# Gated mix of sliding attention and a GEGLU block: two staging tiles moved from ring s to rings s and c

## The chip, the cores and the metric

The kernel runs on one core of a Trainium2 chip. The metric is the device time of one execution in microseconds, as the median of several runs; one more execution is taken by the hardware profiler. Five engines work side by side and meet at semaphores: TensorE (PE), VectorE (DVE), ScalarE (ACT), GpSimd (POOL) and SyncE (SP), the last of which here only issues DMAs.

## The reference

The inputs are x (2048 tokens of 512 channels), weights for attention and for a gated feed-forward block (FFN), and a gate vector:

```python
def _A_ref(x, wqkv, wo):          # 32 heads of 16, 8 keys per token, every second token back
    qkv = ...(x @ wqkv)
    idx = pos[:, None] - (jnp.arange(8) * 2)[None, :]
    logits = jnp.einsum("bhsd,bhswd->bhsw", q, k[..., idx, :]) * scale   # masked where idx < 0
    attn = softmax(logits)
    return (einsum("bhsw,bhswd->bhsd", attn, v[..., idx, :])) @ wo
def _B_ref(x, w_gate, w_up, w_down):   # 512 -> 1792 -> 512
    return (_gelu(x @ w_gate) * (x @ w_up)) @ w_down
g = _sigmoid((x * gate_w).sum(-1, keepdims=True))
return g * a + (1 - g) * b
```

## The kernel before

Tokens are split by parity (`par` 0 and 1), since the attention looks back by even steps only: two problems of 1024 tokens. Every matrix product is made in full precision from three products of high and low parts, and with a two-by-two block scheme that saves multiplications at the price of sums between the blocks (the names `a11`, `b21`, `t3`, `s4` and so on are blocks and sums of blocks).

For each parity the program first makes keys and queries, then runs `ffn(par)`: fourteen blocks `f` of 128 hidden channels. `gate_up` makes the gate and the up product of a block (L558 on PE), `hidden` multiplies them and splits the product into the high part `hh` and the low part `hl` (L572, L574, L575), and `down` (L601) multiplies those with the down weights `d`. The operands `g0` and `g1` of a block are split into high and low parts by ACT (L515, L520) with a subtraction by a POOL DMA (L516); `d` by L544, L545 and L547, for the first two blocks by `down_split` (L117 and DVE).

The product with the value weights, `values(par)`, has no stage of its own: its steps are cut into the first two FFN blocks, in the order that the table `PLAN` gives. It works by token tiles `t` of 0 to 3. Each makes two sets of 128 rows of values (`jj = t` and `jj = BT + t`), 512 channels wide, in two halves of 256. ACT (L224) and DVE (L232) gather each set in one tile of 512 columns in SBUF, and two DMAs write it to memory, its first half by L228 (on ACT's queue for par 0, on SP's for par 1) and its second half by L233 (on SP's queue). The table `STAGES` says from which ring each of these tiles is taken: `STAGES[t][0]` for the first set, `STAGES[t][1]` for the second.

A ring is a small set of equal buffers under one name, handed out in turn: a new tile waits until every reader of the tile that had its buffer is done, DMAs included. The rings `s` and `c` have four buffers each. `c` tiles are 544 columns wide, `s` tiles 512. Each FFN block takes two tiles of `s`, the copies of `p5` and `u2` out of PSUM (`copy`, L563), and four of `c`: the gelu of the first half (`c11`, L656), the sums `c12` and `c22` (`add`, L568), and the gelu of the second half (`ge`, L675).

The attention runs on DVE beside all of this (scores L324 and L327, softmax L344 to L368, mix L386 to L401), fed in between the FFN steps by `pull`. Its results go through memory and come back by L806, are split by L87 and L88, and are multiplied with the output weights (L828) at the end. The end of the program is a run of L828 matmuls.

The order of the instructions on each engine is not the order of the text: a scheduler takes the whole program, estimates when each instruction could run, and writes out the order of each engine; it hands out the ring buffers as it goes. A ring that is changed can move instructions on all engines.

Of the kernel before, what the change touches and what calls it, by code (L numbers as in the profile page):

```python
# [48 lines left out]
def tile_gated_mix(ctx: ExitStack, tc: tile.TileContext, xt, wqkv, wff, wo, out):  # L49
# [11 lines left out]
    def tl(tag, dt=F32):  # L61
        return pool.tile([P, COLS.get(tag, 512)], dt, name=tag, bufs=BUFS[tag])
# [14 lines left out]
    for i in range(WARM):  # L77
        c = i // 4 % 2 * QW
# [115 lines left out]
            VR["t4"] = VR["b21"]  # L194
            sub(VR["t4"], VR["b21"], VR["t2"])

    STAGES = (("r", "r"), ("hh", "hl"), ("s", "s"), ("s", "s"))

    def value_steps(par, t):

# [14 lines left out]
        def staged(i):  # L215
            if ("s", i) not in T:
                T["s", i] = tl(STAGES[t][i])[:, :512]
            return T["s", i]
# [1188 lines left out]
```

## Time and profile before

| what | value |
|---|---|
| median of 3 runs | 606.85 us (605.4 to 607.78) |
| the profiled execution | 601.95 us |
| its span | 600.2 us |
| PE busy | 587.3 us (98%), 2730 matmuls |
| DVE busy | 540.0 us (90%) |
| ACT busy | 391.2 us (65%) |
| POOL busy | 89.2 us (15%) |

A profile line of the timeline reads: start in us, duration, engine, line of the program, operation, output<-input, shapes, count, and in brackets the time that the engine was idle before it and what ended that. In a list of waits the columns are the total, the number of times and the longest. Several consecutive instructions of one kind are one line. The duration given for PE is from the start of the first to the modelled end of the last; matmuls overlap, so that the start of the next line is the better mark.

### The profile page before, as it was taken

The page shows a single profiled execution, that of the slowest core. Times are in us where ns is not written, and L with a number is a line of the kernel's source. Part 1 is how long each engine was busy: PE and PEld are TensorE (multiplying, and loading weights), DVE is VectorE, ACT ScalarE, POOL GpSimd, SP SyncE. Part 2 cuts the span into 40 slices and gives each one's busy share as a digit, 9 for nine tenths or more (in the row PEclk, how much of TensorE's full clock was granted, in tenths as well). Part 3 has the DMA queues.
Part 4 walks back from the last instruction along what each step waited for, and adds up shares of the span by engine and source line. Part 5 has one row for each costly group of instructions (what it writes and reads, how often), then busy time and mean ns, then how long its engine had stood idle before and what let it go on. Part 6 is the DMA issues. An engine that isn't in the chain of part 4 may idle for free.

```text
span 600.2 us, 8102 instructions
## 1 busy us (share of the span) xinstructions
PE 587.3 (98%) x2730; PEld 488.1 (81%) x2730; DVE 540.0 (90%) x644; ACT 391.2 (65%) x678; POOL 89.2 (15%) x121
## 2 busy tenths in 40 slices
PE   8999999999999999999899999999999999999997
PEld 6888978878887888877788888788888888888886
DVE  5998989879999899989989999899999899799972
ACT  5857646787776967785874346768666766785532
POOL 0501002111211111201117000111111111101200
PEclk9999999999999999999999999999999999999999
DMA  8778969898999799896779886877798587737824
GB/s 315 245 233 235 297 195 254 226 287 225 258 254 283 199 274 239 225 331 243 229 220 274 241 211 183 225 210 181 192 236 261 146 219 219 225 95 203 128 66 158
DMA packets 79810, 134.18 MB, mean 224 GB/s; under 512 B 7964, under 2 KB 45210, under 8 KB 79512
## 3 DMA queue, kind: packets, MB, share of 16 engines
q1 hardware_dynamic: 64426, 98.72, 50.0%
q0 software_dynamic: 12576, 32.97, 28.2%
q10 hardware_dynamic: 2766, 1.96, 1.0%
q8 instruction: 21, 0.34, 0.2%
q14 instruction: 21, 0.17, 0.1%
HBM read 68.30 MB, written 38.86 MB: 179 GB/s over the span
## 4 chain that ended last, share of the span: by engine, by line
PE 86%; DMA 5%; issue 4%; ACT 2%; DVE 2%; POOL 0%; SPq 0%; DVEq 0%; POOLq 0%; ACTq 0%
PE p L558 40%; PE p L601 11%; PE acc L601 10%; PE acc L895 7%; PE p L895 5%; PE p L828 5%; PE acc L210 5%; PE acc L828 2%; DMA g<-raw 2%; DMA vs<-s 1%; DMA d<-r 1%; DMA raw<-xt 1%; ACT L675 0%; ACT L344 0%; DVE prod L386 0%
## 5 line engine op out<-in xcount | busy, mean ns | idle before, releaser
L558 PE MATMUL p<-S,g 128*128 128x512 f32 x672 | 168.9, 390 | 3.7 <-ACT s L563 2.7
L558 PEld LDWEIGHTS p<-S,g 128*128 128x128 f32 x672 | 125.0, 188 | 30.3 <-ACT s L563 3.4
L558 PE MATMUL p<-A,g 128*128 128x512 f32 x504 | 128.9, 390 | 1.1 <-DMA g<-raw 0.5
L558 PEld LDWEIGHTS p<-A,g 128*128 128x128 f32 x504 | 93.6, 188 | 21.3 <-DVE c L568 1.2
L327 DVE TENSOR_REDUCE lg<-prod 128x128 f32<-128x2048 f32 x32 | 73.0, 2281 | 0.1
L516 POOL DMA_DIRECT2D g<-raw x40 | 34.5, 862 | 227.7 <-ACT g L515 134.0
L601 PE MATMUL p<-d,hh 128*128 128x512 f32 x224 | 67.4, 389 | 0.0
L601 PE MATMUL acc<-d,hh 128*128 128x512 f32 x224 | 62.1, 390 | 0.7 <-DMA d<-r 0.7
L386 DVE TENSOR_TENSOR prod<-kq,lg 128x2048 f32<-128x2048 f32 x24 | 54.7, 2277 | 0.2
L601 PEld LDWEIGHTS acc<-d,hh 128*128 128x128 f32 x224 | 41.8, 188 | 9.7 <-DMA d<-r 1.1
L601 PEld LDWEIGHTS p<-d,hh 128*128 128x128 f32 x224 | 42.1, 188 | 8.8
L563 ACT ACTIVATE s<-p 128x512 f32<-128x512 f32 x56 | 32.9, 597 | 22.9 <-PE p L558 18.8
L520 ACT ACTIVATE g<-raw 128x1024 fp32r<-128x1024 f32 (+1 forms) x40 | 39.5, 987 | 12.1 <-PE p L558 9.4
L515 ACT ACTIVATE g<-raw 128x1024 fp32r<-128x1024 f32 (+1 forms) x40 | 39.3, 986 | 10.3 <-PE p L895 6.3
L545 POOL DMA_DIRECT2D d<-r x24 | 20.5, 855 | 147.0 <-ACT d L544 120.1
L601 PE MATMUL p<-d,hl 128*128 128x512 f32 x112 | 41.8, 389 | 0.0
L574 ACT ACTIVATE hh<-c 128x512 fp32r<-128x512 f32 x56 | 35.1, 628 | 9.9 <-DVE c L572 9.9
L575 DVE TENSOR_TENSOR hl<-c,hh 128x512 fp32r<-128x512 f32 x56 | 38.3, 683 | 3.7 <-ACT hh L574 3.6
L568 DVE TENSOR_TENSOR c<-p,s 128x512 f32<-128x512 f32 x56 | 38.1, 683 | 3.8 <-PE p L558 2.8
L572 DVE TENSOR_TENSOR c<-c 128x512 f32<-128x512 f32 x56 | 38.2, 682 | 2.2 <-ACT c L675 2.1
L617 ACT ACTIVATE rt<-p 128x512 f32<-128x512 f32 x48 | 27.7, 595 | 18.6 <-PE p L601 18.0
L390 DVE TENSOR_TENSOR prod<-prod 128x1024 f32<-128x1024 f32 x32 | 38.9, 1216 | 0.1
(203 smaller groups left out, 1016.0 us busy)
## 6 DMA issues: line engine op xcount, KB each, us to landing
g<-raw POOLq DMA_DIRECT2D x27, 512.0 KB, 6.1
raw<-wff SPq DMA_DIRECT2D x42, 256.0 KB, 4.0
ws<-g SPq DMA_DIRECT2D x14, 768.0 KB, 5.7
g<-ws SPq DMA_DIRECT2D x14, 768.0 KB, 5.3
r<-wff SPq DMA_DIRECT2D x28, 256.0 KB, 4.2
d<-r POOLq DMA_DIRECT2D x24, 256.0 KB, 6.2
g<-raw POOLq DMA_DIRECT2D x13, 384.0 KB, 6.3
os<-tb SPq DMA_DIRECT2D x64, 64.0 KB, 4.3
```

The lines of the kernel that those rows point to most:

```text
L327: nc.vector.tensor_reduce(two_of(lg, jj), prod.rearrange("p j w (h d) -> p (j w) h d", d=DH), axis=AX.X, op=OP.add)
L386: paced(nc.vector.tensor_tensor(prod.rearrange("p j w (h d) -> p (j w) h d", d=DH), spans(v, jj).rearrange("p j w (h d) -> p j w h d", d=D ...
L390: nc.vector.tensor_tensor(prod[:, :, :4], prod[:, :, :4], prod[:, :, 4:], op=OP.add)
L515: nc.scalar.activation(lo, raw, AF.Copy, scale=-1.0)
L520: ins = nc.scalar.activation(hi, raw, AF.Copy)
L558: LAST[:] = [nc.tensor.matmul(ps, w_, a_, start=(start and kc == 0 and n == 0), stop=(kc == 1 and n == 2), skip_group_check=True)]
L568: nc.vector.tensor_tensor(c, ps, s, op=OP.add)
L572: nc.vector.tensor_tensor(ge, ge, up, op=OP.mult)
L575: nc.vector.tensor_tensor(hl_, ge, hh_.bitcast(F32), op=OP.subtract)
L601: ins = nc.tensor.matmul(pp, a[:, ts], w, start=(i == 0 and n == 0 and gr == 0), stop=(i == 1 and n == 2), skip_group_check=True)
L828: ins = nc.tensor.matmul(pa, a, b, start=(first and n == 0), stop=(last and n == 2), skip_group_check=True)
L895: return lambda *args, **kw: self.add(getattr(self.eng, name)(*args, **kw))
```

## The change

Token tile 2 takes its first tile from `s` and its second from `c`; token tile 3 its first from `c` and its second from `s`. Both took both from `s`.

```diff
-    STAGES = (("r", "r"), ("hh", "hl"), ("s", "s"), ("s", "s"))
+    STAGES = (("r", "r"), ("hh", "hl"), ("s", "c"), ("c", "s"))
```

The instructions are the same in kind and number. Their order differs on every engine from 74 us on. Three places follow; numbers behind a name tell the tiles of one name apart, `[waits ...]` names the engines or DMA queues on which an instruction waits.

The first place is in par 0, between blocks 1 and 2. On PE, `p_847` and `p_888` belong to block 1, `p_1035` to block 2, `acc0` to `acc3` to the values or to `down`; the names behind `<-` are the operands. Before, block 1's matmuls from `S_247` stood behind the first of block 2, from `g0_842`:

```order
L558 MATMUL p_1035<-A_118,g0_842 128x512 [waits Activation_49]
L558 MATMUL p_1035<-A_118,g0_842 128x512
L558 MATMUL p_1035<-A_118,g0_842 128x512 [waits DMASW2_49]
L558 MATMUL p_1035<-A_119,g0_842 128x512 x3
L558 MATMUL p_847<-S_247,g1_708 128x512 [waits Activation_49]
L558 MATMUL p_847<-S_247,g1_708 128x512 x2
L558 MATMUL p_847<-S_248,g1_708 128x512 x3
L601 MATMUL acc0_1050<-d_952,hh_798 128x512 [waits PE_49,Activation_49]
L601 MATMUL acc0_1050<-d_952,hh_798 128x512
```

Now they stand 30 rows earlier, straight behind those from `S_245`:

```order
L558 MATMUL p_888<-S_245,g1_708 128x512 [waits Activation_49]
L558 MATMUL p_888<-S_245,g1_708 128x512 x2
L558 MATMUL p_888<-S_246,g1_708 128x512 x3
L558 MATMUL p_847<-S_247,g1_708 128x512 [waits Activation_49]
L558 MATMUL p_847<-S_247,g1_708 128x512 x2
L558 MATMUL p_847<-S_248,g1_708 128x512 x3
L210 MATMUL acc0_775<-hh_468,S_247 128x256 [waits Activation_49]
L210 MATMUL acc0_775<-hh_468,S_247 128x256
```

On ACT at the same place, `s_895` and `s_939` are the copies `p5` and `u2` of block 1, `s_808`, `s_929`, `s_836` and `s_948` stage tiles. Before, `g0_842` (the high part of block 2's operand) stood ahead of `s_939`, and `s_939` and the first eviction into `s_948` waited for DMAs:

```order
L224 ACTIVATE s_929<-acc3_876 128x256 [waits PE_49]
L117 ACTIVATE d_952<-r_785 128x512 [waits PE_49]
L117 ACTIVATE d_955<-r_838 128x512 [waits DMAHW6_49]
L520 ACTIVATE g0_842<-raw_632 128x768
L563 ACTIVATE s_939<-p_847 128x512 [waits DMAHW6_49,DMAHW3_49,DVE_49]
L224 ACTIVATE s_836<-acc0_775 128x256 [waits DVE_49,PE_49]
L224 ACTIVATE z_113<-acc0_775 128x1
L228 DMA vs00_86<-s_836 128x2x128 [waits DMAHW2_49,Activation_49]
L638 ACTIVATE p_1042<-p_1035 128x512 [waits PE_49]
L224 ACTIVATE s_948<-acc2_941 128x256 [waits DMAHW7_49,DMAHW2_49]
```

Now the stage tiles are `s_808`, `c_836`, `c_929` and `s_948`; the gelu `c_907` is the `ge` of block 0, `c_965` the `c11` of block 1. In two pieces, a little apart:

```order
L675 ACTIVATE c_907<-p_594 128x512
L515 ACTIVATE g1_897<-raw_632 128x1024 [waits DVE_49]
L228 DMA vs00_86<-hl_729 128x2x128 [waits DMAHW1_49,Activation_49]
L224 ACTIVATE s_808<-acc1_782 128x256 [waits PE_49]
L224 ACTIVATE z_113<-acc1_782 128x1
L563 ACTIVATE s_895<-p_888 128x512
L563 ACTIVATE s_939<-p_847 128x512
```

```order
L574 ACTIVATE hh_910<-c_907 128x512 [waits DVE_49]
L224 ACTIVATE acc1_883<-acc3_876 128x258 [waits PE_49,Activation_49]
L224 ACTIVATE c_929<-acc1_883 128x256 [waits PE_49]
L224 ACTIVATE z_113<-acc1_883 128x1
L656 ACTIVATE c_965<-p_854 128x512
L228 DMA vs00_86<-c_929 128x2x128 [waits DMAHW7_49,Activation_49]
L224 ACTIVATE s_948<-acc2_941 128x256 [waits PE_49]
L117 ACTIVATE d_952<-r_785 128x512 [waits DMAHW3_49]
L117 ACTIVATE d_955<-r_838 128x512
L520 ACTIVATE g0_842<-raw_632 128x768
```

The two L563 copies stand one behind the other and wait for no DMA; ahead of the L520 copy of `g0_842` stand `s_939` and `s_948`. Further on come `c_1076`, the `ge` of block 1, and `c_1111`, the `c11` of block 2, both with waits for DMAs that read the stage tiles whose buffers they take:

```order
L675 ACTIVATE c_1076<-p_847 128x512 [waits DMAHW1_49,DMAHW0_49,PE_49]
L515 ACTIVATE g1_1091<-raw_885 128x1024 [waits DMAHW4_49,DMASW1_49,DVE_49]
L656 ACTIVATE c_1111<-p_1042 128x512 [waits DMAHW7_49,DMAHW6_49]
L520 ACTIVATE g1_1091<-raw_885 128x1024
L228 DMA vs00_86<-s_948 128x2x128 [waits Activation_49]
```

The second place is on ACT towards the end of par 0, at 254 us of the profile before: an exp of the attention (L344) with its table load, a gelu (L675) with another, and the L638 copy of `p_2530`, for which PE waits there. Before:

```order
L895 ACTIVATE A_2550<-raw_2384 128x512 [waits DMAHW6_49,PE_49]
L544 ACTIVATE d_2532<-r_2382 128x512 [waits PE_49]
L895 ACTIVATE A_2552<-raw_2384 128x512
L344 ACT_TABLE_LOAD
L344 ACTIVATE lg_2204<-lg_2204 128x512 [waits DVE_49]
L675 ACT_TABLE_LOAD
L675 ACTIVATE c_2565<-p_2389 128x512 [waits PE_49]
L638 ACTIVATE p_2530<-p_2523 128x512 [waits Activation_49]
L617 ACTIVATE rt_1133<-p_2473 128x512 [waits PE_49]
L617 ACTIVATE rt_1157<-p_2502 128x512 [waits PE_49]
```

Now:

```order
L547 ACTIVATE d_2532<-r_2382 128x512 [waits DMAHW4_49,DMASW1_49,PE_49]
L344 ACT_TABLE_LOAD
L344 ACTIVATE lg_2204<-lg_2204 128x512 [waits DVE_49]
L617 ACTIVATE rt_1133<-p_2473 128x512 [waits PE_49]
L617 ACTIVATE rt_1157<-p_2502 128x512 [waits PE_49,Activation_49]
L895 ACTIVATE A_2550<-raw_2384 128x512 [waits DMAHW6_49,PE_49]
L638 ACTIVATE p_2530<-p_2523 128x512 [waits PE_49,Activation_49]
L544 ACTIVATE d_2532<-r_2382 128x512
L895 ACTIVATE A_2552<-raw_2384 128x512
L675 ACT_TABLE_LOAD
L675 ACTIVATE c_2565<-p_2389 128x512 [waits PE_49]
```

The exp stands ahead of the copies into `A`, and the gelu with its table load behind the L638 copy.

The third place is on PE at the change of parity, at 282 us of the profile before. `p<-d` are the last matmuls of `down`, whose results ACT evicts by L612; `acc<-g_2556` and `p<-g_2593` are the first products of keys and queries of par 1 (L895). Before:

```order
L601 MATMUL p<-d,hh 128x512 x2
L601 MATMUL p<-d,hl 128x512
L895 MATMUL acc_2796<-g_2556,A 128x512 x6
L895 MATMUL acc_2797<-g_2556,A 128x512 x6
L895 MATMUL acc_2798<-g_2556,A 128x512 x6
L601 MATMUL p<-d,hh 128x512 x8
L895 MATMUL acc_2799<-g_2556,A 128x512 x6
L601 MATMUL p<-d,hl 128x512 x4
L895 MATMUL p<-g_2593,A 128x512 x5
L895 MATMUL p<-c,A 128x512
```

Now:

```order
L601 MATMUL p<-d,hh 128x512 x8
L601 MATMUL p<-d,hl 128x512 x4
L895 MATMUL acc_2796<-g_2556,A 128x512 x6
L895 MATMUL acc_2797<-g_2556,A 128x512 x6
L895 MATMUL acc_2798<-g_2556,A 128x512 x6
L895 MATMUL acc_2799<-g_2556,A 128x512 x6
L895 MATMUL p<-g_2593,A 128x512 x5
L895 MATMUL p<-c,A 128x512
```

The twelve `p<-d` matmuls stand ahead of the 24 of `acc<-g_2556`, and no longer between them and `p<-g_2593`.

In par 1 the first place is repeated with SP in place of ACT as the queue of the L228 DMAs. There the L568 sums `c_3605` and `c_3711` on DVE carry waits for DMAs that read stage tiles, and the L563 copies beside the stages carry none.

## Prediction

> **What bounds the kernel now.** I read the busy times first, then what TensorE (PE) waited for, then the timeline around each of those waits, and last the final microseconds. From the page, PE's waits (total, times, longest), one stretch of the stages table, and the chain's last pieces:
>
> ```profile
> PE 587.3 (98%) x2730; PEld 488.1 (81%) x2730; DVE 540.0 (90%) x644; ACT 391.2 (65%) x678; POOL 89.2 (15%) x121
> ...
> PE p L558 <- ACT s L563: 2.7, 2, 1.5
> PE p L895 <- ACT p L895: 2.3, 1, 2.3
> ...
> PE p L558 <- ACT p L638: 0.9, 1, 0.9
> PE acc L601 <- DMA d<-r: 0.7, 1, 0.7
> PE p L558 <- DMA g<-raw: 0.5, 1, 0.5
> PE p L558 <- DVE c L568: 0.5, 1, 0.5
> ...
> 60.00:110.00 50.00, 48.53 (x267) 41.86 (x266) 46.38 (x51) 30.07 (x58) 6.80 (x8) 1.00 0.89 248
> ...
> 585.71 5.44 PE acc L828 x24
> 591.14 5.45 PE p L828 x24
> ```
>
> PE is the bound: 24 matmuls of 512 columns take 5.44 us in the last row but one, 0.2267 each, and the granted clock is 1.00 even in the stretch with the longest ring wait. So PE's sum of matmuls is fixed, and the change can act only on the few gaps between them. It adds and removes no instruction. The first wait in the list, 2.7 us in two places, is the one that ring s causes: an L563 copy into s that waits for a stage's DMA.
>
> I size each gap by starts: start of a group plus its matmuls at 0.2267 (0.12 for 256 columns, 356.13 to 356.85 below) is when PE would be free; the next start less that is what was lost. The first half of the sequence (par 0), with ACT beside it:
>
> ```profile
> 80.50 1.61 PE L558 MATMUL p<-A,g 128*128 128x512 f32 x6
> 83.58 1.65 PE L558 MATMUL p<-S,g 128*128 128x512 f32 x6 [1.47 <-ACT s L563]
> ...
> 79.57 0.83 ACT L520 ACTIVATE g<-raw 128x768 fp32r<-128x768 f32 x1
> 82.92 0.60 ACT L563 ACTIVATE s<-p 128x512 f32<-128x512 f32 x1 [2.53 <-DMA vs<-s]
> 83.42 0.38 ACT L224 ACTIVATE s<-acc 128x256 f32<-128x256 f32 x1
> 83.83 0.37 ACTq L228 DMA_DIRECT2D vs<-s  x1
> ...
> 76.39 6.43 DMA vs<-s
> ```
>
> Free at 80.50 + 6 x 0.2267 = 81.86, started at 83.58: 1.72 lost. The copy sat 2.53 us until a stage DMA of 6.43 us had left the buffer. The other gaps that the new order touches:
>
> ```profile
> 132.79 0.84 PE L558 MATMUL p<-A,g 128*128 128x512 f32 x3
> 134.16 1.19 PE L558 MATMUL p<-A,g 128*128 128x512 f32 x4 [0.53 <-DVE c L568]
> ...
> 192.32 0.61 PE L558 MATMUL p<-A,g 128*128 128x512 f32 x2
> 193.47 0.73 PE L558 MATMUL p<-A,g 128*128 128x512 f32 x2 [0.54 <-DMA g<-raw]
> ...
> 257.54 0.84 PE L601 MATMUL acc<-d,hl 128*128 128x512 f32 x3
> 259.33 1.66 PE L558 MATMUL p<-S,g 128*128 128x512 f32 x6 [0.95 <-ACT p L638]
> ...
> 283.88 1.07 PE L601 MATMUL p<-d,hl 128*128 128x512 f32 x4
> 287.26 0.96 PE L895 MATMUL p<-g,A 128*128 128x512 f32 x3 [2.32 <-ACT p L895]
> ...
> 356.13 0.89 PE L210 MATMUL acc<-d,S 128*128 128x258 f32 x6
> 356.85 0.87 PE L210 MATMUL acc<-rt,S 128*128 128x256 f32 x6
> 358.99 1.65 PE L558 MATMUL p<-S,g 128*128 128x512 f32 x6 [1.27 <-ACT s L563]
> ...
> 380.36 1.07 PE L601 MATMUL acc<-d,hh 128*128 128x512 f32 x4
> 382.12 1.21 PE L601 MATMUL acc<-d,hh 128*128 128x512 f32 x4 [0.70 <-DMA d<-r]
> ```
>
> By the same arithmetic they lost 0.69 (at 133), 0.70 (192), 1.11 (258), 2.47 (284), 1.42 (357, the second ring-s wait, par 1) and 0.85 (381). With the 1.72 that is 8.96 us, the most that this change could ever take away.
>
> **The change part by part.** All terms are against the profiled execution: 601.95 us, 0.8% below the median of 606.85, so the sum is scaled by 606.85 / 601.95 at the end.
>
> *Ring s, par 0.* Four stage tiles took all four s buffers; now two do. The two L563 copies of block 1, s_895 and s_939, carry no DMA wait any more and stand side by side on ACT, and the six matmuls p_847<-S_247 have moved 30 rows forward on PE. The 1.72 goes. What is late next is the hi copy of g0_842 (L520), which the matmuls p_1035 wait for. It ended at 79.57 + 0.83 = 80.40, just ahead of PE's 80.50, so it has no cover. In the new row one L563 copy (0.60) and one L224 eviction (0.38) stand ahead of it that did not, and another L224 eviction (0.38) has gone behind. Bounds of the new gap: 0 if ACT's idle time there takes them up, 1.7 if it costs what the old wait did. I take 1.0, near 0.60 + 0.38, since the eviction ahead waits on PE itself. Net -0.72.
>
> *Ring c, par 0.* Stage tiles c_836 and c_929 now hold the buffers that the gelu outputs c_1076 (L675, block 1) and c_1111 (L656, block 2) take next, and these two wait for the stages' DMAs. The spread of such transfers (issue to landing: min, median, max, first of L233 and then of L228), and when the two gelus ran before:
>
> ```profile
> DMA to landing us min/median/max: 1.8/4.8/9.5
> ...
> DMA to landing us min/median/max: 2.0/4.1/8.9
> ...
> 91.73 0.60 ACT L675 ACTIVATE c<-p 128x512 f32<-128x512 f32 x1 [0.38 <-PE p L558]
> ```
>
> The last DMA from that tile went out at 83.83; a median landing frees the buffer at 87.9, the longest at 92.7, 1.0 us after the gelu wants it; an operand copy like that of 79.57, but wider, stands ahead of the DMA now, about one more. Cost taken 0, because the median still leaves nearly 3 us; bounds 0 and 2.0.
>
> *Par 1.* The 1.42 goes in the same way. There the stages' second-half DMAs are all on SP, in a new order, and the L568 sums c_3605 and c_3711 on DVE wait for them; behind those on DVE stand hidden products for PE. Bounds 0 (median landing) and 1.7 (what the old wait cost in par 0). I take a third of the wait that is replaced, 0.5, since these DMAs queue behind loads on SP. Net -0.92.
>
> *The rows in between.* The scheduler hands out the changed rings and gives PE, ACT and DVE another order from 74 us to the end of par 0 and again in par 1. At 284 the twelve matmuls into p from d have moved ahead of the 24 of acc<-g_2556. PE waited for ACT there:
>
> ```profile
> 284.30 2.42 ACT L612 ACTIVATE rt<-p,gc 128x512 f32<-128x512 f32 x4 [3.82 <-PE p L601]
> 286.60 1.09 ACT L895 ACTIVATE p<-acc 128x512 f32<-128x512 f32 x2
> ...
> 254.83 1.28 ACT L344 ACT_TABLE_LOAD   x1
> ...
> 256.78 1.28 ACT L675 ACT_TABLE_LOAD   x1
> 258.70 0.58 ACT L638 ACTIVATE p<-p 128x512 f32<-128x512 f32 x1
> ```
>
> Four evictions (2.42) and half of 1.09 make 2.96, now under 24 x 0.2267 = 5.44 of matmuls: the 2.47 goes, -2.47. Bounds 0 and -2.47. At 258 the exp and its table load stand earlier, and the second load (1.28) and its gelu come after the L638 copy on which PE waited: -1.11, bounds 0 and -1.11. At 381 the L544 copy that starts the late DMA stands earlier on ACT: -0.85, bounds 0 and -0.85. The gaps at 133 and 192 I could not place in the new order: 0, bounds 0 and -1.39. Against this, a new order makes gaps of its own. The old one had two of about 0.7 in this stretch that no ring explains (133, 192), so I charge two more at 0.75: +1.5, bounds 0 and +3.0.
>
> *The end.* PE's last 24 matmuls, at 591.14, need the last attention tile:
>
> ```profile
> 588.42 0.69 DVE L88 TENSOR_TENSOR hl<-raw,hh 128x512 fp32r<-128x512 f32 x1 [6.50 <-ACT hh L87]
> ...
> 345.00:583.00 238.00, 236.04 (x1076) 196.22 (x1075) 221.82 (x240) 153.65 (x254) 28.32 (x34) 1.00 0.72 188
> ```
>
> It is ready at 589.11, 2.0 us early. So of the terms so far (-0.72 - 0.92 - 2.47 - 1.11 - 0.85 + 1.5 = -4.57) only 2.0 is free; the other 2.6 must be made good by DVE, which is idle 238.00 - 221.82 = 16.2 us from 345 on, in part behind PE. I take two thirds made good: +0.9 lost, bounds 0 and 2.6.
>
> Sum: -4.57 + 0.9 = -3.67, 598.28 us, and scaled to the median 603.1.
>
> [...]
>
> **The rivals.** (1) No difference: the attention chain on DVE does not come earlier, so the last tile is ready at 589.11 as before and the end gains only 2.0: 599.95, scaled 604.8. For it speaks DVE's 90%; against it, that DVE also waits on PE. The change not doing what it says, the ring wait merely moved, ends here as well: 284 and 258 alone are 3.58, less 1.5 of new gaps, 604.8 again.
> (2) Slower: ring c. It carries four tiles per FFN block where s carries two, and its gelus stand in ACT's row with the operand copies behind them. With a landing of 9.5 for 6.43, a wait like the old one costs PE 1.72 + 3.07 = 4.8. Two of the four new waits at that size make +9.6 on -4.17: 607.4, scaled 612.3. It decides from about 7.2 us of such waits (4.17 and the 3.0 that can be told), one and a half of them. Against it stand the medians above.
> [...]
>
> **How the numbers follow.** Forecast 0.52, rival 1 0.31, rival 2 0.17. A measurement of this kernel can tell about 0.5%, 3.0 us, from no change, and the three cases are the three outcomes: faster 0.52, same 0.31, slower 0.17. The time is the forecast's 603.1. The low end, 599.0, is the forecast without charge for new gaps, par-1 waits and the end (-6.57, scaled 600.2) and most of 133 and 192 besides; the high end, 609.0, takes in rival 1 and the milder half of rival 2.
>
> **What would show it.** Right: PE's waits name no L563 with a stage DMA behind it; no gap of 2.3 at the L895 copies near 284; L520 of g0_842 starts after PE has come to p_1035. Wrong: L675, L656 or L568 into c waiting on vs<-c; the last tile's hl with PE idle before the final 24 matmuls; several new gaps over 1 us between 85 and 400.

## The result

The changed kernel takes 599.97 us (median of 4 runs, 597.96 to 601.31) against 606.42 (605.40 to 607.78): ratio 0.9889, 95% interval 0.9854 to 0.9924. In a second comparison it was 599.40 against 604.10: 0.9943, 0.9920 to 0.9966. So it is faster, by 4.7 to 6.5 us as the medians have it and by 3.4 to 6.7 us as the ratios have it; 603.1 was forecast, a ratio of 0.9938 to the 606.85 it started from. Spreads, medians and mean clocks below are over all runs, while the ratios leave out those more than 1.5% above the fastest of their kernel. A ratio is not the quotient of two medians of the table: for tile 2 only, where they differ most, that quotient is 0.9925.

The profiled executions differ far less, 599.73 against 601.95. The page of after, and all that PE waited for:

```profile
PE 587.9 (98%) x2730; PEld 489.8 (82%) x2730; DVE 538.9 (90%) x644; ACT 392.0 (66%) x678; POOL 89.4 (15%) x121
...
PE acc L601 <- DMA d<-r: 1.9, 1, 1.9
PE acc L210 <- ACT acc L224: 1.1, 1, 1.1
PE p L79 <- DVE zero L73: 1.1, 1, 1.1
PE p L558 <- ACT p L638: 0.9, 1, 0.9
PE p L558 <- DVE c L568: 0.9, 2, 0.5
PE acc L895 <- DVE A L895: 0.4, 1, 0.4
PE p L558 <- ACT g L520: 0.2, 1, 0.2
```

No L563 and no L895 copy is left in the list; every wait but the two of the start is in a new place. Their places in the timeline of after, three rows of ACT at 381 us, and the waits of an L563 copy in ring s on ACT and of a sum in ring c on DVE:

```profile
82.59 0.39 PE L601 MATMUL acc<-d,hh 128*128 128x512 f32 x1
83.22 0.96 PE L558 MATMUL p<-A,g 128*128 128x512 f32 x3 [0.24 <-ACT g L520]
...
105.23 0.61 PE L601 MATMUL p<-d,hl 128*128 128x512 f32 x2
107.75 0.97 PE L601 MATMUL acc<-d,hh 128*128 128x512 f32 x3 [1.91 <-DMA d<-r]
...
268.87 0.39 PE L601 MATMUL p<-d,hl 128*128 128x512 f32 x1
269.80 1.43 PE L558 MATMUL p<-A,g 128*128 128x512 f32 x5 [0.54 <-DVE c L568]
...
319.28 0.64 PE L210 MATMUL acc<-d,A 128*128 128x258 f32 x4
320.99 0.99 PE L210 MATMUL acc<-d,S 128*128 128x258 f32 x6 [1.08 <-ACT acc L224]
...
379.30 1.07 PE L601 MATMUL acc<-d,hl 128*128 128x512 f32 x4
381.27 0.98 PE L558 MATMUL p<-S,g 128*128 128x512 f32 x3 [0.90 <-ACT p L638]
...
378.80 1.28 ACT L344 ACT_TABLE_LOAD   x1
380.10 0.63 ACT L344 ACTIVATE lg<-lg 128x512 f32<-128x512 f32 x1
380.64 0.58 ACT L638 ACTIVATE p<-p 128x512 f32<-128x512 f32 x1
...
525.83 1.29 PE L558 MATMUL p<-A,g 128*128 128x512 f32 x5
527.45 0.73 PE L558 MATMUL p<-A,g 128*128 128x512 f32 x2 [0.32 <-DVE c L568]
...
360.01 1.09 ACT L563 ACTIVATE s<-p 128x512 f32<-128x512 f32 x2 [0.69 <-DMA vs<-s]
360.42 0.69 DVE L568 TENSOR_TENSOR c<-p,s 128x512 f32<-128x512 f32 x1 [1.30 <-DMA vs<-c]
```

By starts, as in the prediction, these gaps are 0.40 (at 83), 2.07 (105), 0.70 (269), 1.23 (320), 1.06 (381) and 0.49 (527): 5.95 us in place of 8.96, or 3.0 less. The profiled executions differ by 2.2, since after's first 60 matmuls, which the change leaves alone, took 1.5 us longer this time: eight of them stood 0.43 us apart from 6.7 us on, behind a gap of only 0.5 us, though the granted clock reads 1.00 there. Why was not tried. The second profile of after, 598.91 us, lies 3.0 below the first of before.

So the traces leave 1.7 to 3.5 us of the medians unexplained. Two things were open: why before's runs lie so far above its profile, and whether the gain belongs to the rings or to the order.

### The profile page after: what moved, and what is told of

Same layout as the page of the kernel before. It is cut to its first block, busy times and chain, and to the rows that moved or that the text cites. A ratio compares the mean times of both kernels' runs of the same rounds, so it can differ in the third digit from the quotient of the medians.

```text
span 597.9 us, 8098 instructions
## 1 busy us (share of the span) xinstructions
PE 587.9 (98%) x2730; PEld 489.8 (82%) x2730; DVE 538.9 (90%) x644; ACT 392.0 (66%) x678; POOL 89.4 (15%) x121
## 4 chain that ended last, share of the span: by engine, by line
PE 90%; DVE 3%; DMA 2%; ACT 2%; issue 2%; POOL 0%; SPq 0%; POOLq 0%; ACTq 0%; DVEq 0%
PE p L558 41%; PE p L601 11%; PE acc L601 11%; PE acc L895 8%; PE acc L210 6%; PE p L895 5%; PE p L828 5%; PE acc L828 2%; DMA d<-r 1%; DMA raw<-xt 1%; DVE prod L386 1%; DVE prod L390 1%; DVE A L895 0%; DVE c L568 0%; DVE c L572 0%
## 5 line engine op out<-in xcount | busy, mean ns | idle before, releaser
L520 ACT ACTIVATE g<-raw 128x1024 fp32r<-128x1024 f32 (+1 forms) x40 | 39.6, 991 | 11.3 <-PE p L558 11.1
L563 ACT ACTIVATE s<-p 128x512 f32<-128x512 f32 x56 | 32.9, 599 | 18.9 <-PE p L558 17.8
L568 DVE TENSOR_TENSOR c<-p,s 128x512 f32<-128x512 f32 x56 | 37.8, 683 | 7.2 <-PE p L558 4.7
L617 ACT ACTIVATE rt<-p 128x512 f32<-128x512 f32 x48 | 27.5, 593 | 18.4 <-PE p L601 18.3
```

The source lines that it names most:

```text
L520: ins = nc.scalar.activation(hi, raw, AF.Copy)
L568: nc.vector.tensor_tensor(c, ps, s, op=OP.add)
```

## The experiments

| kernel | ratio to before (95%) | median | lowest to highest | runs | mean granted clock |
|---|---|---|---|---|---|
| before, in three comparisons | | 604.58 | 599.74 to 610.85 | 99 | 0.9961 |
| before, once more | 1.0021 (0.9991 to 1.0050) | 605.34 | 601.14 to 610.50 | 12 | 0.9959 |
| changed, once more | 0.9943 (0.9920 to 0.9966) | 599.40 | 598.78 to 600.48 | 7 | 0.9991 |
| change in par 0 only | 0.9987 (0.9962 to 1.0012) | 603.29 | 598.20 to 607.71 | 12 | 0.9968 |
| change in par 1 only | 0.9993 (0.9973 to 1.0013) | 603.57 | 601.88 to 604.48 | 12 | 0.9978 |
| before, L895 behind `down` | 0.9969 (0.9948 to 0.9990) | 603.42 | 601.07 to 610.55 | 12 | 0.9965 |
| changed, early L544 | 0.9881 (0.9855 to 0.9907) | 597.76 | 597.37 to 599.12 | 6 | 0.9998 |
| tiles in hl and hh | 0.9945 (0.9918 to 0.9972) | 602.04 | 600.12 to 604.08 | 12 | 0.9977 |
| tile 2 only | 0.9959 (0.9935 to 0.9982) | 599.94 | 597.93 to 603.14 | 12 | 0.9968 |
| before, pace 0.80 | 0.9977 (0.9945 to 1.0008) | 603.30 | 598.53 to 607.54 | 12 | 0.9957 |
| changed, pace 0.80 | 0.9987 (0.9960 to 1.0014) | 602.95 | 601.16 to 604.49 | 12 | 0.9983 |
| early L544, and hl and hh in par 1 | 0.9938 (0.9915 to 0.9960) | 599.98 | 598.91 to 602.25 | 12 | 0.9985 |

(The 99 runs are those of before that stood beside the others, and its own twelve of the next row.)

**Both kernels once more.** No edit.

> The kernel before, once more. Its profiled execution (601.95 us) lies 4.5 us under the median of its runs (606.42), while the changed kernel's profiled execution (599.73) lies at its median (599.97); so the two traces explain 2.2 of 6.45 us. Theory A: most runs of before hold a wait of 3 to 5 us that the first profiled execution was spared; then this profile is near 606 and shows a gap on PE that the first has not. Theory B: the spread is even over many small gaps; then the profile again shows gaps of 9 us in all between 74 and 400 us, and the rest is nowhere in particular. Ratio to before: 1.000 within 0.004.

> The changed kernel, once more. Both theories: ratio 0.985 to 0.993. If the new DMA wait that its trace shows at 105 us (2.07 us, the lo part of a down weight) is by chance, it is absent or under 1 us here; if it belongs to the new order, it is 1.5 to 2.5 us again.

Before's second profile took 605.43 us, 3.5 more than its first, and shows where. The gap at 285 us is the same; what follows is not (the last three rows are a table by stretches; the column behind POOL's is the granted clock):

```profile
284.67 1.07 PE L601 MATMUL p<-d,hl 128*128 128x512 f32 x4
288.06 1.63 PE L895 MATMUL p<-g,A 128*128 128x512 f32 x5 [2.32 <-ACT p L895]
...
288.00:288.60 0.60, 0.54 (x2) 0.48 (x3) 0.40 (x1) 0.60 (x3) 0.43 (x2) 1.00 0.76 222
288.60:292.50 3.90, 3.90 (x12) 3.02 (x11) 3.40 (x5) 3.90 (x9) 0.76 (x1) 0.57 1.01 336
292.50:296.00 3.50, 3.50 (x17) 2.85 (x16) 3.50 (x7) 2.42 (x5) 0.00 (x0) 1.00 0.36 141
```

Twelve matmuls in 3.9 us instead of 17: the granted clock was 0.57 in this stretch just behind the gap, and 1.00 in those before and after it. The 24 matmuls behind the gap took 7.22 us from first start to the next group's, 5.62 in the first profile: 1.6 us lost. The first profile had the same gap and 1.00 throughout. This is half of Theory A: most runs hold something that the first profile was spared, but it is not one wait. The second thing is the DMA for the down weight at 381 us, whose wait was 0.70 in the first profile (the two L563 waits grew too, from 2.7 to 3.2 us in all):

```profile
385.80 1.20 PE L601 MATMUL acc<-d,hh 128*128 128x512 f32 x4 [1.95 <-DMA d<-r]
...
378.24 7.52 DMA d<-r
```

The changed kernel's ratio came out a little over the expected range, at 0.9943. Its gap at 105 us was 2.16 us again (by starts), so that one belongs to the new order.

**One parity at a time.** `STAGES` is taken as changed for one value of `par`, as before for the other:

```diff
-    STAGES = (("r", "r"), ("hh", "hl"), ("s", "s"), ("s", "s"))
+    STAGES = (("r", "r"), ("hh", "hl"), ("s", "s"), ("s", "s"), ("s", "c"), ("c", "s"))
...
-                T["s", i] = tl(STAGES[t][i])[:, :512]
+                T["s", i] = tl(STAGES[t + 2 if par == 0 and t > 1 else t][i])[:, :512]
```

> The change in the first token parity alone. On PE the order is that of the changed kernel up to the middle of the second parity's values. Theory A (the gain sits in the first parity: ring wait 1.72, the gaps at 258 and 284 us of 1.11 and 2.47, and what before's usual runs lose there besides): ratio 0.988 to 0.993. Rival (the gain is shared by the two ring waits evenly): ratio 0.993 to 0.997.

> The change in the second token parity alone; up to 310 us the order is that of the kernel before. Theory A: the second parity's part is the ring wait of 1.42 against new gaps of about the same sum, so 0.997 to 1.003. Rival: 0.993 to 0.997.

Theory A missed for par 0: no gain that can be measured. Its profile has lost the ring wait and the gaps at 258 and 285 and has the new DMA wait of after, here with a slow stretch behind it (first row, a stretch); and the ring-s wait of par 1 is still there, 1.0 us:

```profile
106.40:109.60 3.20, 3.20 (x8) 2.53 (x9) 2.62 (x3) 0.90 (x2) 0.86 (x1) 0.52 1.08 279
...
PE acc L601 <- DMA d<-r: 2.3, 2, 2.0
...
PE p L558 <- ACT s L563: 1.0, 1, 1.0
```

Its runs spread over 9.5 us, as before's do. The change in par 1 alone gains no more in the median, as theory A had it, but its runs lie within 2.6 us. The two halves do not add up to the whole: medians 0.8 and 0.5 under before against 4.7 for both.

**The clock by itself.** Bursts of matmuls with a gap of known length between them; ACT makes the gap:

```diff
+            for m in range(burst):
+                mm = nc.tensor.matmul(pa, w[:, :128], w[:, 128:640], start=True, stop=True, ...)
+                if m == 0 and n > 1:
+                    after(mm, act)
+            act = nc.scalar.activation(junk[:, :width], raw[:, :width], AF.Copy)
+            after(act, last)
```

> No part of the reference is computed: bursts of 44 to 60 matmuls of 512 columns, with an ACT copy between that PE waits for, six widths of it twelve times, so that PE's gap is about 1.0, 1.4, 1.7, 2.0, 2.4 and 2.8 us. Theory: behind gaps under about 1.7 us the next matmuls keep 0.2267 us from start to start, behind the longer ones they stand 0.43 apart for some 3 us in a share of cases that grows with the gap. Rival (the slow stretches have nothing to do with the gaps): no slow matmuls, or as many behind the short gaps.

| gap by starts, us | 0.99 to 1.05 | 1.37 | 1.63 | 1.95 | 2.27 | 2.59 |
|---|---|---|---|---|---|---|
| slow matmuls behind it | 0 of 12 | 0 of 12 | 0 of 12 | 3 of 12 | 8 of 12 | 8 of 11 |

Where it was slow, eight or nine matmuls were slowed, most of them to 0.43 us. They began with one of the first seven behind the gap, up to 1.6 us after its end, and cost 1.55 to 1.64 us against a burst without them, whatever the gap's length. Two gaps in a row, the first without and the second with it, as timeline and as stretches:

```profile
320.96 10.49 PE L42 MATMUL pa<-w 128*128 128x512 f32 x45 [1.79 <-ACT junk L48]
333.56 13.68 PE L42 MATMUL pa<-w 128*128 128x512 f32 x52 [2.11 <-ACT junk L48]
...
320.90:324.40 3.50, 3.44 (x15) 2.87 (x16) 0.01 (x1) 0.00 (x0) 1.00 0.00 0
333.50:336.90 3.40, 3.33 (x8) 2.65 (x9) 0.01 (x1) 0.00 (x0) 0.53 0.00 0
```

The theory holds, the rival falls. The granted clock was 0.53 in the slow stretch of the rows above (333.5 to 336.9 us) and 1.00 in the other, and eight matmuls 0.43 us apart make a slow stretch some 3.4 us long. A gap of 1.95 us was followed by one in a quarter of the cases, of 2.27 us in 8 of 12, and none of the 36 gaps up to 1.63 us was.

The whole kernels agree with the bursts. Their thirteen profiles hold nine stretches of 512-column matmuls 0.43 us apart behind the first 11 us, and each of them follows a gap of 2.1 to 5.3 us by starts.

**The gap at 285 us alone.** In before, the first L895 matmul of par 1 is ordered behind the last of `down`:

```diff
+        HOLD[:] = [LAST[-1]]
         block(U, "a11", "b11", True, ask=ASK[0])
...
         LAST[:] = [mms.matmul(ps, a[:, t * P:(t + 1) * P], w, start=first, stop=last, skip_group_check=True)]
+        if HOLD:
+            ordered(LAST[-1], HOLD.pop())
```

> The kernel before with one thing of the changed kernel's order: the first product of the second parity (L895) stands behind all matmuls of the last down, so that PE has 5.4 us of work while ACT evicts. STAGES is as before. Theory (a PE wait of over 2 us costs its own length and often a slower clock behind it): the gap of 2.6 us at 285 is gone, the granted clock of most runs is 0.998 or more, and the median falls by 3 to 4.5 us: ratio 0.9925 to 0.995. Rival (a gap costs its length alone): 2.5 us, ratio 0.9955 to 0.9965, with the same spread of clocks as before, 0.992 to 1.0.

The run lies outside both ranges, at 0.9969. The gap went from 285 and a larger one came at 276: without L895 matmuls to do, PE waits for ACT's hh copy, which stands behind copies for par 1:

```profile
275.84 0.39 PE L601 MATMUL p<-d,hl 128*128 128x512 f32 x1
278.87 1.59 PE L601 MATMUL p<-d,hh 128*128 128x512 f32 x5 [2.64 <-ACT hh L574]
```

The cover of 24 matmuls that the prediction counted for L612 was borrowed from the hh copy. In the changed kernel ACT's order fits to it, here it does not, so this run could not price the gap alone.

**The early copy.** In the changed kernel, the L544 copy for block 2's down weight comes one step earlier; the orders of PE and ACT are otherwise almost those of the changed kernel:

```diff
-                    at(4 if f == 2 else 0 if f % 2 and not par else 2, next, steps, None)
+                    at(3 if f == 2 and not par else 4 if f == 2 else 0 if f % 2 and not par else 2, next, steps, None)
```

> The changed kernel with one copy moved: L544 of block 2's down weight is issued one step earlier in the text, so that its POOL DMA starts about 8 us earlier and PE has nothing to wait for at 105 us. Theory: the gap of 2.2 us there is gone and with it the last one long enough to slow the clock: 1.8 to 2.8 us faster than the changed kernel, ratio to before 0.988 to 0.992, clock 0.999 or 1.0 in all runs. Rival (the lo part of block 3's operand, queued behind it on POOL, is late instead): the gap moves by a few us and the ratio stays at 0.993 to 0.996.

The mechanism is the theory's: the clock is 0.999 or 1.0 in all six runs, and the DMA starts at 90.18 us instead of 100.47. The median of 597.76 us is 1.6 under the changed kernel's 599.40; since the two stood beside different runs of before (605.02 and 604.10), the ratios give more, 0.9881 against 0.9943, which is 3.7 us. The 1.8 to 2.8 us of the theory lie between. The wait for d<-r is gone, and the longest that PE still has is 1.1 us:

```profile
PE p L558 <- DVE c L568: 1.1, 3, 0.5
PE acc L210 <- ACT acc L224: 1.1, 1, 1.1
PE p L79 <- DVE zero L73: 1.1, 1, 1.1
PE p L558 <- ACT p L638: 0.9, 1, 0.9
```

This is the fastest version of the study, and its runs lie within 1.8 us.

**Other rings, one tile.** `STAGES` ends in `("s", "hl"), ("hh", "s")`; then in `("s", "c"), ("s", "s")`:

> The two tiles go to hl and hh in place of ring c: STAGES ends in (s, hl), (hh, s). Ring s is relieved as in the change, c is not touched. Theory (ring s and the luck of the new order, not ring c, make the result): the two L563 waits are gone, 3.1 us, other gaps differ, ratio 0.988 to 0.998. Rival (the order that ring c gives is what counts): 0.998 or over.

> Only token tile 2 is changed: (s, c), then (s, s). In both parities the L563 copy that waited for a stage DMA waits no more; the first eviction of tile 3 into s still waits. Theory (gaps over 1.9 us and the slow clock behind them decide; the ring-s waits are DMA waits whose length differs from run to run): the two ring-s gaps (1.7 and 1.4 us) are gone; if the gap at 285 us stays, clocks stay at 0.996 to 1.0 and the ratio is 0.993 to 0.998; if it goes too, 0.988 to 0.993. Rival (both tiles are needed): 0.998 or over.

Both ratios fall within the theory's first ranges, though some clocks of the second are lower than it said, down to 0.993. Both have lost the two L563 waits and kept the 2.3 us wait for the L895 copy; hl and hh also show one of 2.1 for g<-raw, tile 2 one of 1.7. A gain of this size does not need ring c, nor both tiles; but each of these edits draws an order of its own too.

**A new order alone.** `pull(0.77)` becomes `pull(0.8)`, in before and in the changed kernel:

> The kernel before with the pace of the value steps at 0.80 for 0.77: the rings and both L563 waits are those of before, but the order from 130 us on is drawn anew. Theory: the two ring-s gaps stay, and with them a wide spread of times; what a new order alone does is within 0.5%: ratio 0.995 to 1.005. Rival (the gain of the change is the luck of a new order): 0.985 to 0.993.

> The changed kernel with the same new pace, 0.80 for 0.77; the order from 130 us on is drawn anew. Theory: no ring-s gap, narrow spread, ratio to before 0.985 to 0.995. Rival (luck of the order): no better than before, 0.996 to 1.004.

For before the theory's range held (0.9977). For the changed kernel it failed and the rival held: with the same rings and another order on PE from 152 us on, 0.9987, no gain that can be measured. Its profile has the wait at 104 us again and new ones for a copy (L617) and for g<-raw:

```profile
PE acc L601 <- DMA d<-r: 2.0, 1, 2.0
PE p L558 <- ACT rt L617: 1.7, 1, 1.7
PE p L558 <- DMA g<-raw: 1.1, 2, 0.9
```

The profile of before at pace 0.80 fell on the longest of its runs, 607.54 us, and shows what such a run holds: the DMA for the down weight at 380 us, 10.04 us long, and slow matmuls behind it, seven in 3.16 us from start to start (a granted clock of 0.991 over the whole run).

```profile
379.55 0.39 PE L601 MATMUL acc<-d,hh 128*128 128x512 f32 x1
385.09 3.35 PE L601 MATMUL acc<-d,hh 128*128 128x512 f32 x7 [5.15 <-DMA d<-r]
...
375.01 10.04 DMA d<-r
```

**Both edits.** The early copy, and hl and hh in par 1:

```diff
-    STAGES = (("r", "r"), ("hh", "hl"), ("s", "c"), ("c", "s"))
+    STAGES = (("r", "r"), ("hh", "hl"), ("s", "c"), ("c", "s"), ("s", "hl"), ("hh", "s"))
...
-                T["s", i] = tl(STAGES[t][i])[:, :512]
+                T["s", i] = tl(STAGES[t + 2 * par if t > 1 else t][i])[:, :512]
```

> The version with the early copy of block 2's down weight, and in the second parity hl and hh in place of ring c, so that no L568 sum waits for a stage DMA there. Theory: the gap of 1.2 us at 378 us, the one that ring c costs, is gone: 0.5 to 1.5 us faster than with the early copy alone, ratio 0.9855 to 0.9875, clock 1.0. Rival (hh or hl runs short, or the new order brings a gap of its own): 0.988 to 0.992.

Slower than the early copy alone, as the rival had it, and by more: 0.9938 lies above its 0.992. The theory's premise was wrong. Its gap at 378 us was not the price of ring c: as in the changed kernel at 381, PE waited there for an L638 copy that stands behind an exp and its table load on ACT. At 378 us the new order has a wait of 2.23 us for an L617 copy instead, and six of its twelve runs have a clock of 0.997:

```profile
379.97 2.50 PE L558 MATMUL p<-S,g 128*128 128x512 f32 x5 [2.23 <-ACT rt L617]
```

**What the gain is made of.** Among runs with a clock of 0.999 or more, by the author's estimate too high for a slow stretch (1.6 us in 600; before's second profile, with one, has 0.997), before has 601.95 us (20 runs) and the changed kernel 599.28 (8 of its 11): 2.7 us of waits. The mean clocks, 0.9961 and 0.9989, differ by 0.0028, which over 600 us is 1.7 us, about one slow stretch more per run of before. Together that is 4.4 of the 4.85 us between the medians of all these runs (604.58 and 599.73).

How much of this belongs to the rings and how much to the order is not settled. Six kernels have lost both ring-s waits of PE; five of them are faster than before, with ratios of 0.9881 to 0.9959, and the sixth, the changed kernel at pace 0.80, is not. With the rings of before, one other order gave 0.9977, not distinct from 1, and one 0.9969, a small gain.

What decides the long runs is suggested by the spreads. All four kernels whose `STAGES` are those of before in par 1 (before, par 0 only, L895 behind `down`, before at pace 0.80) have runs over 607 us; none of the seven others goes over 604.5. In those four the POOL DMA for the down weight starts at 375.0 to 378.2 us, some 4.8 to 5.7 us before PE needs it, and their five profiles show 6.0, 6.26, 6.34, 7.52 and 10.04 us for it; in the changed kernel it starts at 371.65 and PE does not wait for it:

```profile
371.65 0.85 POOL L545 DMA_DIRECT2D d<-r  x1 [2.12 <-ACT d L544]
```

That this DMA lengthens a long run is seen in the one profile at 607.54 and inferred for the others. Why it takes now 6 and now 10 us was not tried.

## Why the prediction was right, and where it was off

- Ring s, both parities: PE's two waits for L563 copies went, as said, 3.14 us. In par 1 one L563 copy still waited 0.69 us on ACT for a stage DMA, where the prediction had none, but PE did not wait for it. The new wait for g0_842 came where it was put and cost 0.40, not 1.0.
- Ring c: the gelus of blocks 1 and 2 did not wait (0, as said). In par 1 one L568 sum on DVE waited 1.30 us for a stage DMA, but PE did not wait for that sum: 0 for the 0.5 charged. The DMAs were not quick (those from c tiles took 4.1 to 5.2 us there); PE had other matmuls to do.
- The gaps at 284, 258 and 381 went, as said. The reason given for 284 was incomplete, as the L895 experiment shows. The kind of wait at 258 came back at 381, though: there the exp and its table load now stand ahead of the L638 copy, and PE lost 1.06. At 133 and 192, taken as 0, another 1.39 went.
- New gaps of the order: 5.55 us in five places for the 1.5 charged. This is the term most out of size: it is 4.05 too small, and the other terms together undersold the gain by 3.4. That the sum came out near the traces is in part luck.
- The end: 0.9 was charged because the last tile had only 2.0 us to spare. DVE came forward with PE, the tile was ready at 586.82, and PE asked for it at 588.94, so nothing was lost:

```profile
586.13 0.69 DVE L88 TENSOR_TENSOR hl<-raw,hh 128x512 fp32r<-128x512 f32 x1 [6.56 <-ACT hh L87]
...
588.94 5.45 PE p L828 x24
```

Term by term the sum was -3.67, and two profiles without a slow stretch behind the first 11 us (601.95 and 598.91 us, clocks 1.000 and 0.999) give -3.0. The medians of all runs differ by 4.85: 2.7 us of waits, for which -3.67 was too much, and 1.7 of clock, for which the sum had nothing.

The step that failed was to scale one profiled execution, 601.95 us, to the median of three runs, 606.85, as if the 4.9 us between them were spread evenly. Of these, 2.3 were the draw of three long runs, since the median of 99 is 604.58; from there the forecast's ratio would have given 600.8. The rest was not even either. It was slow stretches of 1.6 us behind gaps that the sum priced at their own length, and a DMA wait at 381 priced at the 0.85 of one execution, where others show 0.4 to 5.3. The prediction took PE's sum of matmuls as fixed, since the granted clock of its trace was 1.00 even beside the longest ring wait; in the second profile the gap at 285 us, 2.48 us by starts, has 0.57 behind it.

Rival 2's mechanism, waits on ring c, appears once and off PE's path. The -4.17 it starts from is the forecast's -3.67 without the 0.5 charged to ring c in par 1; no run shows that term by itself, and the 0.5 turned out 0. Rival 1's, a tail that holds the gain back, does not appear. What came nearest to undoing the gain was a fate that no rival named: another order with the same rings has no gain that can be measured.

## What to carry to other kernels

Where PE is 98% busy, look at the longest single waits first: here none of 36 gaps up to 1.63 us in the bursts had slow matmuls behind it, while 19 of 35 gaps from 1.95 to 2.59 us had, and then cost 1.55 to 1.64 us beyond their length. Before a sum goes on one profile, compare its time and clock with the other runs; if it lies below all of them, the runs hold something that it does not show. And where a scheduler draws the whole order again, a change of 1% needs a control with another order before it is credited to the edit: here the edit gave a ratio of 0.994 with one order and 0.999 with another.

## What the runs showed of the hardware

- In the bursts, slow matmuls (0.43 us for 512 columns, granted clock 0.53 from 333.5 to 336.9 us) followed none of 36 gaps up to 1.63 us, 3 of 12 at 1.95, 8 of 12 at 2.27 and 8 of 11 at 2.59. They cost 1.55 to 1.64 us each time and began up to 1.6 us behind the gap.
- The same POOL DMA of 256 KB, in the same place of four nearly equal programs, took 6.0, 6.26, 6.34, 7.52 and 10.04 us in five executions.
